# A token-major w1 with shifts in its stationary operand, h transposed by DMA, and kv on 64x32 array tiles

## The chip, the core and the metric

The kernel runs on one NeuronCore of one Trainium2 chip. The metric is the device time of one execution, in microseconds (us), as the median of several runs. Beside it stands a profiled execution, in which every instruction of the five engines has a start and a duration: TensorE (PE for matmuls, PEld for loads of the stationary operand), VectorE (DVE), ScalarE (ACT), GpSimd (POOL) and SyncE (SP), which issues most of the DMAs.

## What is computed

The input x has 2048 tokens of 448 numbers (S = 2048, D = 448), in bf16. The reference normalizes it, runs two branches on the normalized xn, and adds both to x:

```python
xn = layernorm(x);  return x + A(xn) + B(xn)

# A: linear attention, 16 heads of 28
q, k, v = heads(xn @ wqkv)
phi(t)  = concat(softmax(t @ w_phi), softmax(-(t @ w_phi)))     # 56 features a head
kv = phi(k).T @ v;  z = sum over tokens of phi(k)
o  = (phi(q) @ kv) / (phi(q) @ z + 1e-6);   A = o @ wo

# B: token-mixing MLP
h  = gelu(layernorm(xn) @ w1)            # 448 columns, four groups of 112
hs = the groups shifted along the tokens by +1, -1, +2, -2 (zeros at the ends)
x1 = xn + hs @ w2
B  = x1 + gelu(layernorm(x1) @ w3) @ w4  # w3: 448 x 1792
```

A shift acts on tokens only, and w1 on columns only, so a group's columns of w1 may be applied to shifted tokens and give the shifted h.

## The kernel before

The tokens form 16 tiles of 128. A layer-norm tile `xn` is token-major (a token a partition). Its transpose `xnT` (features on partitions, tokens along the row) feeds the matmuls. The 448 features are spread over four blocks of 128 partitions with overlaps (the helper `load_lap` loads weights so), and a contraction of 448 is done in seven halves of 64 rows: `lap_pair` gives two lists of matmuls for two outputs, in which the lower 64 rows of the array work for one output and the upper 64 for the other, side by side (`row_pairs`), 4 + 4 matmuls in the first list and 3 + 3 in the second. The second list adds to the banks that the first list wrote with the other half of the array.

The helper `Recorder` takes every operation in program order, finds by tile what it must wait for, and emits five streams of instructions. Each engine executes its own stream in order. That order is written by hand in two `play` lists and in a loop of eight rounds (`for ps in range(8)`). All matmuls have line 203 and all vector operations line 215 in the profile, as these are the lines of the Recorder's helpers; activations have line 211, DMAs 218 (transposing) and 221. So groups are told apart by the names of their tiles. Names that differ in a number only are merged: `w` stands for w1 to w4, `bank` for the PSUM banks.

The work comes in these stages (times from the profiled execution):

- Up to 31 us. DVE normalizes the tiles; `xn_T` transposes tiles 0 to 11 on TensorE into PSUM, and ACT copies the result to `xnT`. `xn_Td` transposes tiles 12 to 15 by DMA. `load_wT` transposes parts of wqkv by DMA into the tile `hi`. The calls `V(i, k)` are the two lists of v for the token tiles i and i+1, followed by `v_out`. `W(g, m, k)` are those of w1 for the token group g (512 tokens) and the column groups m and m+1: the w1 columns are stationary (64 x 112), `xnT` streams 512 columns. `w1_out` is the gelu on ACT, which writes `hT` (feature-major). `FO` folds w_phi into the q and k weights. `load_rest` loads w2, w3, wo and w4 on the SP queue. Four pairs of PSUM banks (0 to 3) are shared: `xn_T(i, b)`, `V` and `W` name their pair as the last number, and a matmul that writes a pair waits until ACT or DVE has read what was there.
- 31 to 69 us, the eight rounds. Round ps does k for two tiles (bank pair 1), its exps (`k_exp`, ACT, into `phik`), q (pair 0) and its exps (`q_exp`, into `eq_lo` for rounds 0 to 3 and `eq_hi` after), and on pair 2 either w2 for two tiles (`w2_pair`, with the shifts in the token offset of `hT`) or v for tiles 12 and 14. `w2_out` adds the result to `xn` on DVE, `k_norm` sums and scales phi(k) on DVE and POOL, and `w2_norm` takes the statistics of the second norm. From round 3 on `kv_tile` accumulates kv for the tiles that are ready, in banks 6 and 7.
- 69 to 84 us. The rest of w2 and kv runs among the first w3 pairs (`a(p)`, `b(p)`). kv then goes through SBUF (`kv_copy`) and one more matmul with a selection matrix (`kv_picks`, `kv_blocks`) into `kvq`, which the numerators need.
- 84 us to the end. w3, w4, wo and the numerators (`num_tile`, first call `N(0)`), and the stores. `g_apply` and `g_T` (a transposing DMA) supply w3's input, `o_T` wo's.

The w1 stage before is ordered by these lines, of which two are quoted:

```python
              W(0, 2, 0), (xn_T, 5, 2), W(0, 0, 1), (xn_T, 6, 3), W(0, 2, 1), (xn_T, 7, 2), (w1_out, 0, 0, 0),
              (w1_out, 0, 2, 1), V(4, 0), V(6, 0), V(4, 1), (v_out, 4, 3), V(6, 1), (v_out, 6, 2),
```

Of the kernel before, what the change touches and what calls it, by code (L numbers as in the profile page):

```python
# [17 lines left out]
class Recorder:  # L18
# [56 lines left out]
    def solve(self):  # L75
# [10 lines left out]
        for eng, fn, w, r, dma, tile in self.ops:  # L86
# [21 lines left out]
            for k in w:  # L108
                if k in writers:
                    want(writers[k], False)  # L110
                if k in readers:
                    want(readers[k], False)
# [111 lines left out]
def bass_parallel_sum__linear_kernel_hedgehog__mixer_s_mlp__prompt_kernel(  # L224
# [7 lines left out]
    CR = 112  # L232
    SHIFTS = [1, -1, 2, -2]
    HW = S + 16
# [3 lines left out]
    with es:  # L238
# [27 lines left out]
        xnT_r = region("xnT", KC * S * 2)  # L266
        xnT = view(xnT_r, KC * S).rearrange("p (c s) -> p c s", c=KC)
        hT_r = region("hT", NM * HW * 2)
        hT = view(hT_r, NM * HW).rearrange("p (m s) -> p m s", m=NM)
# [5 lines left out]
        eq_lo = new("eq_lo", NC * 2 * 1024).rearrange("p (c s f) -> p c s f", c=NC, s=2)  # L275
# [8 lines left out]
        w2 = new("w2", NM * D).rearrange("p (m d) -> p m d", m=NM)  # L284
# [8 lines left out]
        kvT = view(w1_r, 512)  # L293
        kvf = view(w1_r, 512, F32, at=1024)
        pick = view(w1_r, 2 * 128, at=3072).rearrange("p (s c) -> p s c", s=2)
# [92 lines left out]
        R.ew(pool, "memset", hT[:, :, 0:2], 0.0)  # L388
        R.ew(pool, "memset", hT[:, :, S + 2:S + 4], 0.0)
# [32 lines left out]
        def lap(a):  # L422
            return bass.AP(a.tensor, a.offset, [list(a.ap[0]), [192, 2], [1, 256]])

# [105 lines left out]
        def w1_pair(g, m, b):  # L530
            return lap_pair([banks[2 * b + k][0:CR, :] for k in range(2)],
                         lambda k, kc, lo, hi: w1[lo:hi, kc, CR * (m + k):CR * (m + k) + CR],
                         lambda k, kc, lo, hi: xnT[lo:hi, kc, 512 * g:512 * g + 512])

        def w1_out(g, m, b):
            R.act(hT[0:CR, m:m + 2, 2 + 512 * g:2 + 512 * g + 512], two(2 * b)[0:CR, :, :], ACT.Gelu_apprx_tanh)

        def w2_pair(i, b):
            def side(k, lo, hi):
                r = []  # L540
                for m in range(NM):
                    c0 = 2 + 128 * (i + k) - SHIFTS[m]
                    r.append((banks[2 * b + k][:, 0:D], hT[lo:hi, m, c0:c0 + 128], w2[lo:hi, m, :]))
                return r
            return (lambda: row_pairs(side(0, 0, 64), side(1, 64, CR), True),
                    lambda: row_pairs(side(1, 0, 64), side(0, 64, CR)))
# [23 lines left out]
        def kv_tile(i):  # L570
            def side(k, rows):
                return [(banks[6 + k][:, 64 * n:64 * n + HP + DH + 2],
                         phik[rows[0]:rows[1], i, 4 * n:4 * n + 4, :].rearrange("p g e -> p (g e)"),
                         vaug[rows[0]:rows[1], i, 64 * n:64 * n + HP + DH + 2]) for n in range(8)]
            row_pairs(side(0, LO), side(1, HI), i == 0)

        def kv_picks():
            R.ew(pool, "memset", pick[:, :, :], 0.0)
            for q in range(4):
                r = slice(HP * q, HP * q + HP)  # L580
                R.ew(dve, "tensor_copy", pick[r, q % 2, :].rearrange("p (n e) -> p n e", n=4),
                     ident[r, HP * q:HP * q + HP].unsqueeze(1).to_broadcast([HP, 4, HP]))

        def kv_copy():
            n61 = [a.rearrange("p (n e) -> p n e", n=8)[:, :, 0:HP + DH + 2] for a in (banks[6], banks[7], kvf, kvT)]
            R.ew(dve, "tensor_copy", n61[2], n61[0])
            R.ew(dve, "tensor_tensor", n61[3], n61[1], n61[2], op=ALU.add)

        def kv_blocks():
            kt = kvT.rearrange("p (n h e) -> p n h e", n=8, h=2)  # L590
            for s in range(2):
                for k, lo in enumerate((0, 64)):
                    R.mm(banks[6 + k][:, 256 * s:256 * s + 256].rearrange("p (n e) -> p n e", n=8)[:, :, 0:DH + 1],
                         pick[lo:lo + 64, s, :], kt[lo:lo + 64, :, k, 0:DH + 1], s == 0, False)
            for q in range(4):
                r, h, n = slice(HP * q, HP * q + HP), q % 2, 4 * (q // 2)
                src = banks[6 + h][r, :].rearrange("p (s n e) -> p s n e", s=2, n=8)[:, :, n:n + 4, 0:DH + 1]
                dst = kvq[r, :, HP * h:HP * h + DH + 1].rearrange("p (c s) e -> p s c e", s=2)
                if h:
# [140 lines left out]
        for i in range(12, NT):  # L740
            xn_Td(i)
        load_rest()
# [3 lines left out]
        wps = {(g, m): w1_pair(g, m, b) for g, m, b in ((0, 0, 0), (0, 2, 1), (1, 0, 0), (1, 2, 1), (2, 0, 0),  # L746
                                                        (2, 2, 1), (3, 0, 0), (3, 2, 2))}
# [5 lines left out]
        def W(g, m, k):  # L753
            return (wps[g, m][k],)

        def FO(t, m, k):
# [4 lines left out]
              (spin, 2, 256), V(2, 0), (v_out, 0, 2), W(0, 0, 0), (xn_T, 4, 2), V(2, 1), (v_out, 2, 3),  # L761
              W(0, 2, 0), (xn_T, 5, 2), W(0, 0, 1), (xn_T, 6, 3), W(0, 2, 1), (xn_T, 7, 2), (w1_out, 0, 0, 0),
              (w1_out, 0, 2, 1), V(4, 0), V(6, 0), V(4, 1), (v_out, 4, 3), V(6, 1), (v_out, 6, 2),
              W(1, 0, 0), (xn_T, 8, 3, 2), W(1, 2, 0), W(1, 0, 1), (xn_T, 10, 3, 2), W(1, 2, 1),
              (w1_out, 1, 0, 0), (w1_out, 1, 2, 1), V(8, 0), V(10, 0), V(8, 1), (v_out, 8, 2), V(10, 1),
              (v_out, 10, 3), W(2, 0, 0), W(2, 2, 0), FO(1, 0, 0), W(2, 0, 1), (w1_out, 2, 0, 0), FO(1, 0, 1),
              FO(1, 2, 0), W(2, 2, 1), (w1_out, 2, 2, 1), FO(1, 2, 1), W(3, 0, 0), FO(0, 0, 0), W(3, 2, 0),
              FO(0, 0, 1), FO(0, 2, 0), W(3, 2, 1), (w1_out, 3, 2, 2), W(3, 0, 1), (w1_out, 3, 0, 0), FO(0, 2, 1)])
# [8 lines left out]
        kv_picks()  # L777
# [46 lines left out]
        def K(*t):  # L824
            return (lambda: [kv_tile(i) for i in t],)
# [11 lines left out]
        def A(*t):  # L837
# [60 lines left out]
```

## Time and profile before

| | us |
|---|---|
| median of 3 runs (177.82 to 178.65) | 177.84 |
| profiled execution: span of the core (no time of its own beyond the span is on record) | 175.9 |
| PE busy in the span | 170.8 |
| DVE busy | 110.0 |
| POOL busy | 93.7 |
| ACT busy | 82.5 |

The median stands 1.94 us above the profiled span. In the profile, the number after the start in a timeline is how long a merged group lasts, counted to the end of its last instruction; matmuls are pipelined, so the pace is read from the start of one group to the start of the next. "[0.19 <-PE bank L207]" at the end of a line says that the engine had been idle for 0.19 us, and that the named work ended that idle time.

### The profile page before, as it was taken

The page shows a single profiled execution, that of the slowest core. Times are in us where ns is not written, and L with a number is a line of the kernel's source. Part 1 is how long each engine was busy: PE and PEld are TensorE (multiplying, and loading weights), DVE is VectorE, ACT ScalarE, POOL GpSimd, SP SyncE. Part 2 cuts the span into 40 slices and gives each one's busy share as a digit, 9 for nine tenths or more (in the row PEclk, how much of TensorE's full clock was granted, in tenths as well). Part 3 has the DMA queues.
Part 4 walks back from the last instruction along what each step waited for, and adds up shares of the span by engine and source line. Part 5 has one row for each costly group of instructions (what it writes and reads, how often), then busy time and mean ns, then how long its engine had stood idle before and what let it go on. Part 6 is the DMA issues. An engine that isn't in the chain of part 4 may idle for free.

```text
span 175.9 us, 5042 instructions
## 1 busy us (share of the span) xinstructions
PE 170.8 (97%) x2198; PEld 94.7 (54%) x2198; DVE 110.0 (63%) x252; ACT 82.5 (47%) x92; POOL 93.7 (53%) x130
## 2 busy tenths in 40 slices
PE   7899999998999999999999999999999999999993
PEld 4466557744565555665554554554545545545551
DVE  4799906699899697615776981644427415474621
ACT  2368874997779877926324422223214222224000
POOL 3666670016799999860358489460620723523740
PEclk9999999999999999999999999999999999999999
DMA  5994158990001120121011372134611310311331
GB/s 172 330 240 79 35 97 255 390 345 15 0 4 30 34 60 4 30 55 39 4 34 40 79 74 59 48 82 89 93 30 57 82 34 0 86 30 30 86 100 34
DMA packets 32981, 14.87 MB, mean 85 GB/s; under 512 B 24704, under 2 KB 32448, under 8 KB 32960
## 3 DMA queue, kind: packets, MB, share of 16 engines
q1 hardware_dynamic: 30192, 12.64, 29.6%
q10 hardware_dynamic: 2768, 1.92, 3.4%
q8 instruction: 17, 0.28, 0.7%
q14 instruction: 4, 0.03, 0.1%
HBM read 7.08 MB, written 1.84 MB: 51 GB/s over the span
## 4 chain that ended last, share of the span: by engine, by line
PE 91%; DVE 6%; issue 1%; POOL 0%; ACT 0%; DVEq 0%
PE bank L203 90%; DVE vaug L215 1%; DVE st L215 1%; DVE ksum L215 1%; PE bank L207 1%; DVE xn L215 1%; DVE mv L215 0%; ACT xnT L211 0%; POOL rs L215 0%; DVE rks L215 0%; DVEq L176 0%; DVE gT L215 0%; POOL mv L215 0%
## 5 line engine op out<-in xcount | busy, mean ns | idle before, releaser
L211 ACT ACTIVATE phik<-bank 128x1024 bf16<-128x1024 f32 (+1 forms) x44 | 42.3, 984 | 62.4 <-PE bank L203 62.4
L203 PE MATMUL bank<-gT,w 64*128 64x512 bf16 x392 | 50.1, 377 | 0.0
L215 DVE TENSOR_TENSOR vaug<-bank,vaug 128x464 f32<-128x464 f32 (+3 forms) x65 | 32.6, 512 | 23.0 <-PE bank L203 21.4
L203 PE MATMUL bank<-w,phik 64*128 64x448 bf16 (+1 forms) x420 | 45.0, 349 | 0.0
L215 POOL TENSOR_TENSOR xnT<-vaug 128x196 bf16<-128x196 f32 (+1 forms) x32 | 18.1, 585 | 46.8 <-DVE vaug L215 46.8
L203 PEld LDWEIGHTS bank<-w,phik 64*128 64x128 bf16 (+1 forms) x420 | 21.7, 94 | 21.2 <-issue 0.4
L215 POOL TENSOR_TENSOR phik<-phik,rks 128x1792 bf16<-128x1792 bf16 x8 | 25.7, 3212 | 10.8 <-DVE rks L215 10.8
L203 PEld LDWEIGHTS bank<-gT,w 64*128 64x128 bf16 x392 | 18.6, 94 | 17.0 <-ACT hi L211 0.3
L215 POOL TENSOR_TENSOR vaug<-xn,xtok 128x448 f32<-128x448 bf16 x16 | 16.2, 1031 | 0.2 <-DVE vaug L215 0.2
L215 DVE TENSOR_REDUCE ksum<-phik 128x64 f32<-128x1792 bf16 x8 | 16.0, 2006 | 0.0
L203 PE MATMUL bank<-w,hT 64*128 64x448 bf16 (+1 forms) x128 | 15.0, 349 | 0.5 <-DVE vaug L215 0.5
L215 DVE RECIPROCAL vaug<-bank 128x16 f32<-128x16 f32 x16 | 4.1, 257 | 18.0 <-PE bank L203 18.0
L203 PE MATMUL bank<-xnT,wpq 64*128 64x512 bf16 x112 | 14.9, 376 | 0.0
L203 PE MATMUL bank<-xnT,w 64*112 64x512 bf16 x112 | 14.8, 380 | 0.0
L203 PE MATMUL bank<-wpk,xnT 64*128 64x448 bf16 x112 | 13.4, 349 | 0.0
L203 PE MATMUL bank<-wo,xnT 64*128 64x448 bf16 (+1 forms) x106 | 13.4, 349 | 0.0
L215 DVE TENSOR_TENSOR xn<-bank,xn 128x512 bf16<-128x512 f32 (+1 forms) x16 | 9.2, 616 | 6.3 <-PE bank L203 6.3
L203 PE MATMUL bank<-wv,xnT 64*128 64x448 bf16 x112 | 13.0, 350 | 0.1
L215 POOL TENSOR_TENSOR rs<-mv,mhalf 128x1 f32<-128x1 f32 (+2 forms) x18 | 12.2, 679 | 1.5
L215 POOL TENSOR_SCALAR g_tok<-xn,rs 128x512 bf16<-128x512 bf16 x16 | 12.1, 767 | 0.2
L211 ACT ACTIVATE xnT<-bank 128x512 bf16<-128x512 bf16 x12 | 7.0, 603 | 6.3 <-PE bank L207 6.3
L215 DVE BATCH_NORM_STATS2 st<-xtok 128x6 f32<-128x448 bf16 x16 | 9.8, 615 | 0.0
(62 smaller groups left out, 168.0 us busy)
## 6 DMA issues: line engine op xcount, KB each, us to landing
w<-in_B_w_dram SPq DMA_DIRECT2D x2, 896.0 KB, 7.1
out_dram<-vaug SPq DMA_DIRECT2D x15, 112.0 KB, 1.9
w<-in_B_w_dram SPq DMA_DIRECT2D x1, 1568.0 KB, 12.0
xtok<-in_A_x_dram ACTq DMA_DIRECT2D x2, 448.0 KB, 7.3
xtok<-in_A_x_dram SPq DMA_DIRECT2D x2, 224.0 KB, 5.7
w<-in_B_w_dram ACTq DMA_DIRECT2D x2, 224.0 KB, 5.8
wo<-in_A_wo_dram SPq DMA_DIRECT2D x2, 224.0 KB, 8.4
w<-in_B_w_dram SPq DMA_DIRECT2D x1, 392.0 KB, 3.8
```

Source lines behind the costliest of these rows:

```text
L203: self.op("PE", lambda e: e.matmul(out, lhsT, rhs, start=start, stop=stop, skip_group_check=True), [out], [lhsT, rhs], tile=self._tile(lhsT))
L207: self.op("PE", lambda e: e.transpose(out, in_, ident), [out], [in_, ident], tile=self._tile(in_))
L211: self.op("ACT", lambda e: e.activation(out, in_, func, **kw), [out], [in_] + aps)
L215: self.op(eng, lambda e: getattr(e, name)(out, *args, **kw), [out], aps)
```

## The change

w1 becomes token-major. Its stationary operand is `xnT` (64 rows x 128 tokens), read at an offset that holds the shift of the column group, and 112 columns of w1 stream; `xnT` gets 16 zero columns at both ends. A pair of token tiles has 56 matmuls instead of four column groups having 14 per 512 tokens: 448 in all instead of 112. Each gelu covers two token tiles and writes `h_tok` (token-major, in the overlapping layout), which shares its memory with `eq_lo`. A transposing DMA on the SP queue (`h_T`) makes `hT` of each tile, 16 in all. w2 then is an ordinary seven-half contraction (`lap_pair`), 14 matmuls a pair instead of 16. The four `xn_Td` and `load_rest` move in the SP queue behind the first four `h_T` (`bulk`).

kv becomes 512 matmuls of 64 x 32 array tiles, with v stationary (32 columns) and phi(k) streaming 64 columns: eight different tiles of the array in turn (two halves of the rows, four groups of 32 columns). They leave the rounds and stand in two blocks in the third stage, tiles 0 to 11 and 12 to 15. Their banks are zeroed by DVE before. The selection matmul goes; DVE transposes 32 x 32 blocks instead. The Recorder now also waits for readers of PSUM on the same engine.

```diff
-        xnT = view(xnT_r, KC * S).rearrange("p (c s) -> p c s", c=KC)
+        xnT_p = view(xnT_r, KC * HW).rearrange("p (c s) -> p c s", c=KC)
+        xnT = xnT_p[:, :, PAD:PAD + S]
+        hT = new("hT", KC * S).rearrange("p (c s) -> p c s", c=KC)
...
+        eq_lo = view(lo_r, NC * 2 * 1024).rearrange("p (c s f) -> p c s f", c=NC, s=2)
+        h_tok = view(lo_r, NT * 512).rearrange("p (t d) -> p t d", t=NT)
...
-            R.dma(w2[0:CR, :, :], B_w2.rearrange("(m p) d -> p m d", p=CR))
+            load_lap(w2, B_w2)
...
+        def w1_pair(i, b):
+            def side(k, rows, kcs):
+                r = []
+                for kc in kcs:
+                    for m in range(NM):
+                        c0 = PAD + 128 * (i + k) - SHIFTS[m]
+                        c = slice(CR * m, CR * m + CR)
+                        r.append((banks[2 * b + k][:, c], xnT_p[rows[0]:rows[1], kc, c0:c0 + 128],
+                                  w1[rows[0]:rows[1], kc, c]))
+                return r
+            return (lambda: row_pairs(side(0, LO, (0, 1, 2, 3)), side(1, HI, (0, 1, 2, 3)), True),
+                    lambda: row_pairs(side(1, LO, (0, 1, 3)), side(0, HI, (0, 2, 3))))
+
+        def w1_out(i, b):
+            R.act(h_tok[:, i:i + 2, :].rearrange("p t (h e) -> p t h e", h=2), lap2(two(2 * b)), ACT.Gelu_apprx_tanh)
+
+        def h_T(i):
+            R.dma_t(hT[:, :, 128 * i:128 * i + 128], h_tok[:, i, :])
...
+        def kv_tiles(tiles):
+            for i in tiles:
+                for s in range(4):
+                    for k, (lo, hi) in enumerate((LO, HI)):
+                        for q in range(4):
+                            h = 8 * (q // 2) + 2 * s + q % 2
+                            R.mm(banks[6 + k][HP * q:HP * q + HP, 64 * s:64 * s + 64],
+                                 vaug[lo:hi, i, HP * h:HP * h + HP],
+                                 phik[lo:hi, i, 2 * h:2 * h + 2, :].rearrange("p g e -> p (g e)"),
+                                 False, False)
+
+        def kv_copy():
+            R.ew(dve, "tensor_copy", kvf, banks[6][:, 0:256])
+            R.ew(dve, "tensor_tensor", kvT, banks[7][:, 0:256], kvf, op=ALU.add)
+            R.ew(dve, "transpose", kvX, kvT)
...
+        def W(i, k):
+            return (wps[i][k],)
+
+        def WO(i, b):
+            return (lambda: (w1_out(i, b), h_T(i), h_T(i + 1)),)
+
+        def bulk():
+            for i in range(12, NT):
+                xn_Td(i)
+            load_rest()
...
+              (spin, 2, 256), V(2, 0), (v_out, 0, 2), W(0, 0), (xn_T, 4, 2), V(2, 1), (v_out, 2, 3),
+              W(0, 1), WO(0, 0), W(2, 0), (xn_T, 5, 2), W(2, 1), WO(2, 1), (bulk,), (xn_T, 6, 3), (xn_T, 7, 2),
+              V(4, 0), V(6, 0), V(4, 1), (v_out, 4, 3), V(6, 1), (v_out, 6, 2),
+              W(4, 0), W(4, 1), WO(4, 0), (xn_T, 8, 3, 2), W(6, 0), W(6, 1), WO(6, 1), (xn_T, 10, 3, 2),
+              V(8, 0), V(10, 0), V(8, 1), (v_out, 8, 2), V(10, 1),
+              (v_out, 10, 3), W(8, 0), FO(1, 0, 0), W(8, 1), WO(8, 0), FO(1, 0, 1),
+              FO(1, 2, 0), W(10, 0), W(10, 1), WO(10, 1), FO(1, 2, 1), W(12, 0), FO(0, 0, 0), W(12, 1), WO(12, 0),
+              FO(0, 0, 1), FO(0, 2, 0), W(14, 0), W(14, 1), WO(14, 2), FO(0, 2, 1)])
...
-            if ps > 2:
-                kv_tile(2 * ps - 6)
-                kv_tile(2 * ps - 5)
...
-            a(0), (wl[12][0],), b(0), a(1), (w2_last, 12), b(1), K(10, 11, 12, 13),
-            a(2), (wl[14][0],), b(2), a(3), K(14, 15), b(3), (kv_copy,),
-            a(4), (w2_last, 14), b(4), a(5), (kv_blocks,), b(5),
+            a(0), (wl[12][0],), K(*range(12)), b(0), a(1), (w2_last, 12), b(1),
+            a(2), (wl[14][0],), b(2), a(3), K(*range(12, NT)), b(3), (kv_copy,),
+            a(4), (w2_last, 14), b(4), a(5), b(5),
```

More of the change, by code (lines that the diff above doesn't have):

```diff
@@ L111, in solve @@
                 if k in readers:
-                    want(readers[k], False)
+                    want(readers[k], self.rows[k[0]][1])
             if eng == "PE":
@@ L233, in bass_parallel_sum__linear_kernel_hedgehog__mixer_s_mlp__prompt_kernel @@
     SHIFTS = [1, -1, 2, -2]
-    HW = S + 16
+    PAD = 16
+    HW = S + 2 * PAD
     x2d, out2d = A_x[0], out[0]
@@ L265, in bass_parallel_sum__linear_kernel_hedgehog__mixer_s_mlp__prompt_kernel @@
         xn = new("xn", NT * 512).rearrange("p (t d) -> p t d", t=NT)
-        xnT_r = region("xnT", KC * S * 2)
-        xnT = view(xnT_r, KC * S).rearrange("p (c s) -> p c s", c=KC)
-        hT_r = region("hT", NM * HW * 2)
-        hT = view(hT_r, NM * HW).rearrange("p (m s) -> p m s", m=NM)
+        xnT_r = region("xnT", KC * HW * 2)
+        xnT_p = view(xnT_r, KC * HW).rearrange("p (c s) -> p c s", c=KC)
+        xnT = xnT_p[:, :, PAD:PAD + S]
+        hT = new("hT", KC * S).rearrange("p (c s) -> p c s", c=KC)
         phik_r = region("phik", NT * 1024 * 2)
@@ L274, in bass_parallel_sum__linear_kernel_hedgehog__mixer_s_mlp__prompt_kernel @@
         gT = new("gT", 2 * KC * 512).rearrange("p (b c s) -> p b c s", b=2, c=KC)
-        eq_lo = new("eq_lo", NC * 2 * 1024).rearrange("p (c s f) -> p c s f", c=NC, s=2)
+        lo_r = region("lo", NC * 2 * 1024 * 2)
+        eq_lo = view(lo_r, NC * 2 * 1024).rearrange("p (c s f) -> p c s f", c=NC, s=2)
+        h_tok = view(lo_r, NT * 512).rearrange("p (t d) -> p t d", t=NT)
         hi_r = region("hi", NC * 2 * 1024 * 2)
@@ L283, in bass_parallel_sum__linear_kernel_hedgehog__mixer_s_mlp__prompt_kernel @@
         w1 = view(w1_r, KC * D).rearrange("p (c d) -> p c d", c=KC)
-        w2 = new("w2", NM * D).rearrange("p (m d) -> p m d", m=NM)
+        w2 = new("w2", KC * D).rearrange("p (c d) -> p c d", c=KC)
         wo = new("wo", KC * D).rearrange("p (c d) -> p c d", c=KC)
@@ L292, in bass_parallel_sum__linear_kernel_hedgehog__mixer_s_mlp__prompt_kernel @@
         kvq = new("kvq", 8 * 64).rearrange("p (b e) -> p b e", b=8)
-        kvT = view(w1_r, 512)
-        kvf = view(w1_r, 512, F32, at=1024)
-        pick = view(w1_r, 2 * 128, at=3072).rearrange("p (s c) -> p s c", s=2)
+        kvT = view(w1_r, 256)
+        kvX = view(w1_r, 256, at=512)
+        kvf = view(w1_r, 256, F32, at=1024)
         ident = new("ident", 128)
@@ L387, in bass_parallel_sum__linear_kernel_hedgehog__mixer_s_mlp__prompt_kernel @@
         R.ew(pool, "memset", mhalf[:, :], -0.5)
-        R.ew(pool, "memset", hT[:, :, 0:2], 0.0)
-        R.ew(pool, "memset", hT[:, :, S + 2:S + 4], 0.0)
+        R.ew(pool, "memset", xnT_p[:, :, 0:PAD], 0.0)
+        R.ew(pool, "memset", xnT_p[:, :, PAD + S:HW], 0.0)
         busy = gT[:, 0, 0, 0:256]
@@ L423, in lap, with lap2 @@
             return bass.AP(a.tensor, a.offset, [list(a.ap[0]), [192, 2], [1, 256]])
+        def lap2(a):
+            return bass.AP(a.tensor, a.offset, [list(a.ap[0]), [512, 2], [192, 2], [1, 256]])
         def halves(a):
@@ L528, in v_out @@
                 R.ew(dve, "tensor_copy", vd, vs)
[L530 to L536, printed above, removed]
-        def w2_pair(i, b):
[L539 to L546, printed above, removed]
+        def w1_pair(i, b):
[14 more added lines that the diff above has]
+            R.dma_t(hT[:, :, 128 * i:128 * i + 128], h_tok[:, i, :])
+        def w2_pair(i, b):
+            return lap_pair([banks[2 * b + k][:, 0:D] for k in range(2)],
+                            lambda k, kc, lo, hi: hT[lo:hi, kc, 128 * (i + k):128 * (i + k) + 128],
+                            lambda k, kc, lo, hi: w2[lo:hi, kc, :])
         def w2_out(i, b):
@@ L568, in k_norm @@
             R.ew(pool, "tensor_tensor", ph, ph, rk.unsqueeze(2).to_broadcast([128, 4 * H, DH]), op=ALU.mult)
[L570 to L578, printed above, removed]
+        def kv_tiles(tiles):
[8 more added lines that the diff above has]
+                                 False, False)
@@ L579, in kv_picks @@
+        def kv_copy():
+            R.ew(dve, "tensor_copy", kvf, banks[6][:, 0:256])
+            R.ew(dve, "tensor_tensor", kvT, banks[7][:, 0:256], kvf, op=ALU.add)
+            R.ew(dve, "transpose", kvX, kvT)
             for q in range(4):
                 r = slice(HP * q, HP * q + HP)
[L581 to L599, printed above, removed]
+                dst = kvq[r, :, HP * (q % 2):HP * (q % 2) + DH + 1]
@@ L600, in kv_blocks @@
+                src = kvX[r, :].rearrange("p (b e) -> p b e", b=8)[:, :, 0:DH + 1]
+                if q % 2:
                     R.act(dst, src, ACT.Copy)
@@ L739, in bass_parallel_sum__linear_kernel_hedgehog__mixer_s_mlp__prompt_kernel @@
         ln1_apply(dve, 15)
-        for i in range(12, NT):
-            xn_Td(i)
-        load_rest()
         late_3()
         vps = {i: v_pair(i, b) for i, b in ((0, 2), (2, 3), (4, 3), (6, 2), (8, 2), (10, 3))}
-        wps = {(g, m): w1_pair(g, m, b) for g, m, b in ((0, 0, 0), (0, 2, 1), (1, 0, 0), (1, 2, 1), (2, 0, 0),
-                                                        (2, 2, 1), (3, 0, 0), (3, 2, 2))}
+        wps = {i: w1_pair(i, b) for i, b in ((0, 0), (2, 1), (4, 0), (6, 1), (8, 0), (10, 1), (12, 0), (14, 2))}
         fps = {(t, m): fold_pair(t, m, b) for t, m, b in ((1, 0, 2), (1, 2, 3), (0, 0, 1), (0, 2, 3))}
@@ L751, in V @@
             return (vps[i][k],)
-        def W(g, m, k):
-            return (wps[g, m][k],)
+        def W(i, k):
[6 more added lines that the diff above has]
+            load_rest()
         def FO(t, m, k):
@@ L760, in bass_parallel_sum__linear_kernel_hedgehog__mixer_s_mlp__prompt_kernel @@
         play([(xn_T, 0, 0), (spin, 3, 256), (xn_T, 1, 1), (spin, 4, 256), V(0, 0), (xn_T, 2, 0), V(0, 1), (xn_T, 3, 1),
[L761 to L768, printed above, removed]
+              (spin, 2, 256), V(2, 0), (v_out, 0, 2), W(0, 0), (xn_T, 4, 2), V(2, 1), (v_out, 2, 3),
[6 more added lines that the diff above has]
+              FO(0, 0, 1), FO(0, 2, 0), W(14, 0), W(14, 1), WO(14, 2), FO(0, 2, 1)])
         def w2_norm(i):
@@ L776, in bass_parallel_sum__linear_kernel_hedgehog__mixer_s_mlp__prompt_kernel @@
         kv_ones()
-        kv_picks()
+        R.ew(dve, "memset", two(6)[:, :, 0:256], 0.0)
         side = [("w", 0), ("v", 12), ("w", 2), ("w", 4), ("v", 14), ("w", 6), ("w", 8), ("w", 10)]
@@ L824, in K @@
         def K(*t):
-            return (lambda: [kv_tile(i) for i in t],)
+            return (lambda: kv_tiles(t),)
         def w2_last(i):
```

## The prediction

> **What bounds the kernel now.** I read the page first (shares, chain), then busy time by stage, then the timelines of TensorE, ScalarE and the SP queue.
>
> ```profile
> span 175.9 us, 5042 instructions
> ...
> PE 170.8 (97%) x2198; PEld 94.7 (54%) x2198; DVE 110.0 (63%) x252; ACT 82.5 (47%) x92; POOL 93.7 (53%) x130
> ...
> PE 91%; DVE 6%; issue 1%; POOL 0%; ACT 0%; DVEq 0%
> ```
>
> The span is TensorE's: 97% busy and 91% of the chain. By the chain in order of time its one long piece off TensorE after 12 us is DVE's, 35.4 to 41.5. So saved TensorE time counts where nothing else ends later, and any new wait of TensorE counts in full.
>
> ```profile
> 10.66:31.41 20.75, 20.74 (x304) 14.11 (x302) 14.70 (x39) 14.91 (x21) 10.25 (x21) 1.00 0.61 131
> 31.41:68.97 37.56, 37.08 (x519) 20.95 (x515) 31.98 (x54) 30.76 (x34) 26.66 (x18) 1.00 0.29 96
> 68.97:83.55 14.58, 14.58 (x227) 8.85 (x224) 7.65 (x12) 9.63 (x11) 8.12 (x6) 1.00 0.16 37
> ```
>
> Columns: length, then busy time of PE, PEld, DVE, ACT, POOL, clock, DMA. First stage: v, w1 and folds; second: the eight rounds; third: up to the first numerator. In the rounds DVE is busy 32.0 of 37.6 us and ACT 30.8, so they stand close behind TensorE.
>
> ```profile
> 23.88 1.89 PE L203 MATMUL bank<-xnT,w 64*112 64x512 bf16 x16
> 25.61 0.27 PE L203 MATMUL bank<-g_tok,hi 64*128 64x84 bf16 x7
> ...
> 45.11 0.93 PE L203 MATMUL bank<-wpk,xnT 64*128 64x448 bf16 x8
> 45.87 0.62 PE L203 MATMUL bank<-vaug,phik 64*128 64x62 bf16 x32
> 46.32 0.93 PE L203 MATMUL bank<-w,hT 64*128 64x448 bf16 x8
> ```
>
> Start to start gives the pace of two row tiles at once, weight loads included: 16 matmuls of 512 columns in 1.73 us (108 ns each), 8 of 448 in 0.76 (95), 32 of 62 in 0.45 (14.1). Between the last two a column costs 0.21 ns.
>
> ```profile
> 13.57 0.60 ACT L211 ACTIVATE xnT<-bank 128x512 bf16<-128x512 bf16 x1
> 14.36 0.60 ACT L211 ACTIVATE xnT<-bank 128x512 bf16<-128x512 bf16 x1 [0.19 <-PE bank L207]
> 15.15 0.60 ACT L211 ACTIVATE xnT<-bank 128x512 bf16<-128x512 bf16 x1 [0.19 <-PE bank L207]
> 15.64 1.93 ACT L211 ACTIVATE hT<-bank 112x1024 bf16<-112x1024 f32 x2
> ```
>
> ACT copies xnT tiles 5, 6, 7 before the first two gelus; V(4) follows copy 6 at once, at 15.01.
>
> ```profile
> 6.29 10.96 SPq L218 DMA_TRANSPOSE hi<-in_A_wqkv_dram  x8
> 20.57 5.48 SPq L218 DMA_TRANSPOSE xnT<-xn  x4
> 26.09 1.63 SPq L221 DMA_DIRECT2D w<-in_B_w_dram  x3
> 27.76 0.98 SPq L221 DMA_DIRECT2D wo<-in_A_wo_dram  x2
> 28.79 0.47 SPq L221 DMA_DIRECT2D w<-in_B_w_dram  x1
> ```
>
> SP spends 1.3 us on issuing one transposing DMA, 0.53 on a load.
>
> **TensorE work.** w1: 112 x 108 ns = 12.1 us becomes 448 matmuls of 112 columns, 14.1 + 50 x 0.21 = 24.6 ns each, 11.0: -1.1. The new stationary operands start at odd columns; so did w2's before, whose loads took 94 ns like all others, so I charge nothing (a load that did not hide would cost up to 448 x (47 - 25) ns = 10). w2: 16 to 14 matmuls of 95 ns a pair, -0.19 each, -1.1 in the rounds, -0.4 after. kv: 256 x 14.1 = 3.6 us, 2.26 of it in the rounds, 1.39 after, and kv_blocks (0.26) go; 512 matmuls of 64 columns come, all after the rounds. No row shows column tiles. Floor: eight at once, 64 rounds of 29 ns (28.2 for 62 columns, 0.42 a column more), 1.9 us. Ceiling: 512 x 14.2 = 7.3, no concurrency beyond two. Between: 1024 instructions. The page's instruction queue brought 0.28 MB in 17 packets for TensorE's 4396 instructions, 64 B each, 256 a packet, 0.7% of 16 engines' span or 1.2 us a packet; at the floor 256 are used up in 0.47 us, so one or two fetches show. I take 2.9, nearest the floor since loads already run two deep at 14.1.
>
> [...]
>
> **First stage, walked in program order** from W(0) at 10.66 (halves of W 0.79 and 0.59 us, of V 0.76 and 0.57, a transposed tile 0.115, folds 1.0 in all; ACT back to back: copy 0.49, v 0.80, gelu 0.91, with results 0.60, 0.93 and 1.02 after the start; a matmul's result 0.2 after its last start). The gelus now stand before the copies in ACT's queue. gelu(2) needs W(2,1), which ends at 14.3, and runs 14.55 to 15.57; copy 6 behind it ends at 16.06; V(4) writes the bank that copy 6 reads. TensorE, at tile 7 from 14.46, waits 1.5 us in all. Then gelu(4) runs 20.55 to 21.57, copy 8 ends at 22.06, and W(6), whose shifted columns reach into tile 8, waits 1.5. gelu(6) holds copies 10 and 11, V(10) waits 1.25. A fold waits 0.4 for gelu(10). Where the two halves of a W stand together (four places) or nearly so, the second waits for the first's last result on the same bank: 1.1. Work 18.85 + waits 5.8: end at 35.3 instead of 31.4, +3.9. (The same walk over before gives 19.9 of 20.75.)
>
> **SP.** h's 16 transposes go into the queue: four after the wqkv ones (free at 17.25), until 22.45; the xnT ones, until 27.65; seven loads, until 31.3; then h_T(4) to h_T(15), 1.3 us each: h_T(14) is issued at 44.3 and lands 2.45 later, 46.8. Loads before landed in issue order (wo's 224 KB took 8.4 us behind w3, 5.7 in a quieter place), the last at 40.8; now 42.6. So h_T(4) and (6) land at about 42.7 and 43.6 (while the wqkv transposes drained a backlog, they landed 0.45 us apart). The loads come 1.6 us later than before: w2 lands at about 31.5 and is first read at 36.5, w3, wo and w4 have over 20 us of cover, and the first g_T, at 54 before, finds SP free; these cost nothing, and without that cover 1.6. Who waits: eq_lo and h_tok share memory, so q_exp of round 0 must wait for h_T(4) and (6), that of round 1 for h_T(12) and (14); behind them on ACT stand the next k_exp, behind those TensorE's q and k banks.
>
> **Rounds, from 35.3.** A round's TensorE work is 1.33 + 1.33 + 1.51 = 4.17 us without kv. Round 0 loses 0.4 to gelu(14). Round 1's q at 41.95 waits for q_exp(0) until 44.7. From round 2 on DVE is next late: w2_out 1.07, sums and reciprocal 2.5, norms 1.43 make 5.0 in a w2 round, and w2 needs the bank that w2_out reads; this costs 0.9 in round 4, 0.95 in round 7, ACT 0.4 in round 5. Sum 33.4 + 5.4: end at 74.1 instead of 69.0, +5.1. Had the transposes overtaken the loads: 73.1. The 3.4 us taken out of the rounds thus pay for waits.
>
> **Third stage.** 14.58 - 1.39 - 0.26 - 0.4 + 2.9 = 15.4, +0.9. kv's chain of copies (about 2.5 us on DVE and ACT) has 5 us of w3 work beside it, so it costs nothing; without that cover, 2.5. The zeroing of the kv banks on DVE (the nearest rows, 512 elements, take 0.4 to 0.7 us) stands where the four pick copies (0.7) stood, and POOL's two pad memsets (0.15 each) replace two like them: nothing. POOL's last k_norm ends at about 80.5, before tiles 12 to 15 are due at 84. From the first numerator on all is as before.
>
> Sum: 175.9 + 5.1 + 0.9 = 181.9 span. The median of the runs shown, 177.84, stands 1.94 above the span; 183.8 is predicted.
>
> One row more: the clock is granted in full throughout and TensorE's longest idle in these stages is 0.48 us; mine reach 2.75. [...]
>
> **Rivals.** (a) Only one of the waits reaches TensorE. Without the DMA's the rounds end at 72.0, total 181.7; without ACT's the DMA gate alone gives 73.1 and 182.8; if half of each is covered, about 180. For: my latencies are single rows. Chance 0.2. (b) The array tiles do not run side by side, kv costs 7.3: 188.2, or 185 halfway. For: no row shows eight. Against: two tiles start 2 to 8 ns apart. Chance 0.15. (c) Not slower: ACT keeps pace, because TensorE always has other work in hand. It decides whether V(4) starts by 15.2 and q_exp(1) by 41; then rounds run at TensorE's pace, 31.1 + 34.2 + 0.6 of DVE = 65.9, third stage 14.5 to 15.4: 3 us less, 175. For: TensorE is 97% busy and loses 3 us of work. Against: it executes in order and V(4) and W(6) have no cover. Chance 0.08, and 0.05 for a draw of the two effects.
>
> **Numbers.** The forecast has 0.52, with its own range 182.0 to 185.6: the 1.0 between the two landing cases and the 0.8 that the walk leaves open, on both sides. Low 179.0 takes in (a), at its half and with kv at its floor (1.0 less); high 187.7 most of (b). About 0.5% is what a measurement can tell: faster 0.08, same 0.05, slower 0.87.
>
> **Right or wrong shows in:** w1 matmuls of 112 columns at 25 ns start to start; TensorE idle before V(4), W(6) and V(10) put down to ACT's xnT; ACT's first eq_lo exps held until about 42.7 and 46.8 by DMAs; SP full until 47; kv blocks of 384 and 128 matmuls at 4 to 8 ns each. No idle of TensorE between 14 and 31 us would overturn the forecast.

## The result, and the profile after

The changed kernel takes 202.3 us (median of 4, 201.73 to 203.01) against 177.94 for the kernel before on the same chip: 1.136 times as long, interval 1.132 to 1.139. Predicted were 183.8, with a range up to 187.7. The sign and several waits were right; the size was wrong by a factor of four (+24.4 instead of +6.0). In every ratio and its interval below, runs more than 1.5% above the fastest of the same kernel are left out; the medians beside them take in all runs. The page of the changed kernel:

```profile
span 201.0 us, 6204 instructions
...
PE 177.1 (88%) x2770; PEld 94.9 (47%) x2770; DVE 109.7 (55%) x250; ACT 82.6 (41%) x92; POOL 93.6 (47%) x129
...
PEclk9999999969969999995799999999999999999999
...
PE 68%; ACT 9%; DVE 7%; DMA 7%; issue 5%; SPq 2%; POOL 0%; DVEq 0%; ACTq 0%
```

Three things are new. The chain is no longer TensorE's alone: 16% of it is ACT and DMA, and "issue", time in which the engine waits for nothing that the profile shows, is 5% where it was 1%. And the clock line has four slices below 9, at about 40, 57 and 90 to 100 us. TensorE's busy time went up by 6 us although the prediction took work from it; the clock has a large part in that, as 10.4 us of the busy time lie in stretches in which the granted clock was 0.5.

The stretches answer to the three shown of before, with the rest of the span behind them (length, busy PE, PEld, DVE, ACT, POOL, clock, DMA share, GB/s):

```profile
10.86:35.89 25.03, 21.07 (x641) 16.94 (x639) 14.80 (x39) 15.48 (x21) 10.29 (x21) 1.00 0.72 133
35.89:83.98 48.09, 37.96 (x346) 16.64 (x342) 31.84 (x51) 30.20 (x33) 25.46 (x17) 0.93 0.45 107
83.98:108.61 24.63, 19.48 (x634) 10.52 (x633) 7.23 (x13) 9.79 (x11) 8.98 (x6) 0.86 0.13 25
108.61:201.00 92.39, 89.59 (x1084) 45.56 (x1080) 48.55 (x129) 22.79 (x23) 43.13 (x64) 1.00 0.25 56
```

| | before | predicted change | measured change |
|---|---|---|---|
| start | 10.66 | 0 | +0.2 |
| first stage | 20.75 | +3.9 | +4.3 |
| rounds | 37.56 | +1.2 | +10.5 |
| third stage | 14.58 | +0.9 | +10.0 |
| the rest | 92.35 | 0 | 0.0 |

The first stage came out near the walk and the rest of the span as predicted; the rounds and the third stage did not. TensorE's timeline in the first stage (start, length, group, idle time before it):

```profile
15.60 0.42 PE L207 MATMUL bank<-ident,xn 64*128 64x64 bf16 x10 [0.64 <-issue]
16.50 2.82 PE L203 MATMUL bank<-wv,xnT 64*128 64x448 bf16 x28 [0.48 <-ACT xnT L211]
...
22.55 1.73 PE L203 MATMUL bank<-w,xnT 64*128 64x112 bf16 x53 [1.28 <-ACT xnT L211]
...
26.38 2.07 PE L203 MATMUL bank<-wv,xnT 64*128 64x448 bf16 x20 [1.11 <-ACT xnT L211]
```

V(4), W(6) and V(10) wait for ACT's copies, as predicted, and w1's matmuls start 24.5 ns apart (24.6 predicted). Before V(4) a second wait runs beside ACT's: 0.64 us put down to "issue", in the midst of the transposes of tile 6, which the copy needs. Into the rounds lead three rows of SP and three of ACT:

```profile
17.25 6.26 SPq L218 DMA_TRANSPOSE hT<-lo  x4
23.56 5.93 SPq L218 DMA_TRANSPOSE xnT<-xn  x4
...
34.41 22.18 SPq L218 DMA_TRANSPOSE hT<-lo  x12
```

```profile
46.12 1.97 ACT L211 ACTIVATE lo<-bank 128x1024 bf16<-128x1024 f32 x2 [3.57 <-DMA hT<-lo]
...
53.99 1.02 ACT L211 ACTIVATE lo<-bank 128x1024 bf16<-128x1024 f32 x1 [4.28 <-DMA hT<-lo]
56.55 1.02 ACT L211 ACTIVATE lo<-bank 128x1024 bf16<-128x1024 f32 x1 [1.54 <-DMA hT<-lo]
```

The gate that the prediction described is there: q_exp is held until h_T(4) and h_T(14) have landed. But they land at 46.0 and 56.5, not at 42.7 and 46.8. SP spends 22.2 us on twelve transposes, 1.85 each instead of 1.3; the first of them alone is issued from 34.4 to 41.7, behind loads of which the last, w4, lands at 45.5.

The rest is on TensorE:

```profile
39.07 0.74 PE L203 MATMUL bank<-w,hT 64*128 64x448 bf16 x5 [1.46 <-issue]
...
48.15 1.04 PE L203 MATMUL bank<-xnT,wpq 64*128 64x512 bf16 x8 [1.91 <-ACT lo L211]
...
57.63 1.89 PE L203 MATMUL bank<-xnT,wpq 64*128 64x512 bf16 x8 [5.15 <-ACT lo L211]
...
85.70 1.56 PE L203 MATMUL bank<-phik,vaug 64*32 64x64 bf16 x169
89.55 1.21 PE L203 MATMUL bank<-phik,vaug 64*32 64x64 bf16 x128 [2.29 <-issue]
93.55 1.06 PE L203 MATMUL bank<-phik,vaug 64*32 64x64 bf16 x87 [2.79 <-issue]
94.55 3.17 PE L203 MATMUL bank<-gT,w 64*128 64x512 bf16 x14
```

The first kv block, 384 matmuls, takes 8.85 us (85.70 to 94.55), of which 5.1 are two gaps without any releaser. A gap of the same kind, 1.46 us until 39.07, stands at the start of the rounds. Between the two gaps of the block exactly 128 matmuls run, which with their loads are 256 instructions; in the trace the instruction queue (21 packets with 0.34 MB in the whole span) starts packets at 86.9, 90.7 and 94.7. And the work behind such gaps is slow: 14 matmuls that elsewhere last 1.69 us last 3.17, with the clock granted at 0.5 from 91.0 to 97.8. The trace has two more half-clock stretches, of 3.41 us each, from 39.8 and from 56.9.

### The profile page after: what moved, and what is told of

Its sections match the earlier page's. It is cut to its first block, busy times and chain, and to the rows that moved or that the text cites. A ratio compares the mean times of both kernels' runs of the same rounds, so it can differ in the third digit from the quotient of the medians.

```text
span 201.0 us, 6204 instructions
## 1 busy us (share of the span) xinstructions
PE 177.1 (88%) x2770; PEld 94.9 (47%) x2770; DVE 109.7 (55%) x250; ACT 82.6 (41%) x92; POOL 93.6 (47%) x129
## 4 chain that ended last, share of the span: by engine, by line
PE 68%; ACT 9%; DVE 7%; DMA 7%; issue 5%; SPq 2%; POOL 0%; DVEq 0%; ACTq 0%
PE bank L203 67%; DMA hT<-lo 7%; ACT lo L211 4%; DVE xn L215 2%; SPq L218 2%; DVE ksum L215 2%; ACT xnT L211 2%; ACT phik L211 2%; DVE st L215 2%; ACT hi L211 1%; ACT vaug L211 1%; DVE vaug L215 1%; DVE rks L215 1%; DVE mv L215 0%; PE bank L207 0%
## 5 line engine op out<-in xcount | busy, mean ns | idle before, releaser
L203 PE MATMUL bank<-gT,w 64*128 64x512 bf16 x392 | 51.3, 386 | 0.1
L203 PEld LDWEIGHTS bank<-gT,w 64*128 64x128 bf16 x392 | 18.0, 95 | 19.2 <-issue 1.4
L203 PE MATMUL bank<-xnT,wpq 64*128 64x512 bf16 x112 | 17.1, 414 | 7.4 <-ACT lo L211 7.1
L211 ACT ACTIVATE lo<-bank 128x1024 bf16<-128x1024 f32 x16 | 16.1, 1023 | 16.9 <-DMA hT<-lo 9.4
L203 PE MATMUL bank<-w,hT 64*128 64x448 bf16 x112 | 15.1, 374 | 2.2 <-issue 1.5
L203 PE MATMUL bank<-w,xnT 64*128 64x112 bf16 x448 | 14.2, 209 | 1.5 <-ACT xnT L211 1.3
L203 PE MATMUL bank<-wpk,xnT 64*128 64x448 bf16 x112 | 14.0, 356 | 0.0
L203 PEld LDWEIGHTS bank<-w,xnT 64*128 64x128 bf16 x448 | 12.3, 94 | 2.9 <-ACT xnT L211 1.4
L203 PE MATMUL bank<-wo,xnT 64*128 64x448 bf16 (+1 forms) x106 | 13.4, 349 | 0.0
L203 PEld LDWEIGHTS bank<-xnT,wpq 64*128 64x128 bf16 x112 | 5.9, 103 | 15.4 <-ACT lo L211 8.3
```

The source lines that it names most:

```text
L203: self.op("PE", lambda e: e.matmul(out, lhsT, rhs, start=start, stop=stop, skip_group_check=True), [out], [lhsT, rhs], tile=self._tile(lhsT))
L211: self.op("ACT", lambda e: e.activation(out, in_, func, **kw), [out], [in_] + aps)
```

## The experiments

**Theory.** Two independent losses: (Q) the h transposes stand in SP's queue behind the loads and hold ACT through the shared memory of `h_tok` and `eq_lo`; (I) the kv block uses up TensorE's instructions faster than they are brought. Both are enlarged by the clock, granted at 0.5 for 3.41 us from 56.9, in and behind TensorE's wait of 5.15 us until 57.63, and for 6.83 us from 91.0, in and behind the second gap of kv's block. Rivals: the column tiles themselves are slow; the packing of kv into blocks is at fault; ACT's order sets the rounds; the two halves hinder each other.

**The halves apart.** The diff falls into two parts that work alone: kv's (`kv_tiles`, `kv_copy`, the two blocks), and the rest.

> Only the kv half of the change on the kernel before (w1, h and w2 as before). Theory F (instruction supply): the array tiles themselves take about 8 ns a matmul, and the first block stands still for 2 to 3 us at each 256 instructions, put down to issue; about 184.5 us, of it 6 to 7 us in the third stage. Theory C (the column tiles or the change of array mode are slow): the same total, but matmuls slow throughout and no long issue gaps. Theory S (the two halves of the change only hurt together, by the clock): below 181.

> Only the w1, h and w2 half of the change, kv as before. Theory W (waits): +4 us in the first stage for the order on ACT and +10 us in the rounds for transposes of h that come late, clock losses included; about 192 us. If kv were the main cause, below 184. With additive halves the two differences from before sum to 24 us; with theory S clearly less.

Measured: kv alone 187.3 against 178.3, 1.051 (1.048 to 1.055), +9.0 where some 6.5 were expected. w1 alone 1.082 (1.074 to 1.091), median 193.8. By the ratios the halves add 5.1% and 8.2%, together 13.4% before rounding; the whole change adds 13.6% (13.2 to 13.9). No hindrance between the halves shows. With kv alone the gaps are the same, without any h transposes, in TensorE's timeline:

```profile
70.17 2.12 PE L203 MATMUL bank<-phik,vaug 64*32 64x64 bf16 x236
74.73 1.25 PE L203 MATMUL bank<-phik,vaug 64*32 64x64 bf16 x128 [2.44 <-issue]
78.46 0.35 PE L203 MATMUL bank<-phik,vaug 64*32 64x64 bf16 x20 [2.48 <-issue]
78.74 3.13 PE L203 MATMUL bank<-gT,w 64*128 64x512 bf16 x14
```

**kv's parts crossed.** kv's old matmuls (64 x 128 tiles, 62 columns) in the change's two blocks, and the new 64 x 32 tiles in the old places among the rounds:

```diff
-            if ps > 2:
-                kv_tile(2 * ps - 6)
-                kv_tile(2 * ps - 5)
...
+            a(0), (wl[12][0],), K(*range(12)), b(0), a(1), (w2_last, 12), b(1),
```

```diff
+            if ps > 2:
+                kv_tiles((2 * ps - 6, 2 * ps - 5))
...
+            a(0), (wl[12][0],), b(0), a(1), (w2_last, 12), b(1), K(10, 11, 12, 13),
```

> The kernel before with its own kv matmuls (64x128 tiles, 62 columns) put into the two blocks of the change. Theory F: 384 instructions of the first block are used up in 2.7 us, so at least one issue gap of 0.5 to 2.5 us stands in it; 177 to 179.5 us. Theory C: no issue gap, and as the rounds lose 2.3 us of TensorE work that comes back later, 177 to 178.

> The kv half of the change with the new 64x32 matmuls in the places of before: two tiles a round from round 3 on, six tiles after. Theory F: no issue gap over 0.5 us, since a round needs some 210 instructions in 4.7 us; 178 to 179 us, 64 matmuls taking about 0.52 us instead of 0.45. Theory C: 182 to 187, as with the blocks.

Measured: 179.4, 1.007 (1.005 to 1.009), and 179.6, 1.008 (1.005 to 1.011). Neither alone costs much. The old matmuls in a block show no gap at all, where I had expected one of at least 0.5 us; 384 instructions ran in 2.7 us. (The 1.1 us that this run lost I did not trace further.) The new tiles in the old places:

```profile
46.47 0.68 PE L203 MATMUL bank<-phik,vaug 64*32 64x64 bf16 x64
47.09 0.93 PE L203 MATMUL bank<-w,hT 64*128 64x448 bf16 x8
```

64 of them take 0.62 us where 32 of the old took 0.45: the tiles run side by side, but each share of kv costs about a third more than before, +1.3 us over all eight pairs of tiles. So the tiles are no gain, and the 9 us need both together: many instructions at a dense place.

**Which of the two, tiles or instructions?** The old kind of matmul in the blocks, each cut into two of 31 columns: as many instructions as the change has, and no column tile.

```diff
-                return [(banks[6 + k][:, 64 * n:64 * n + HP + DH + 2],
+                return [(banks[6 + k][:, 64 * n + 31 * u:64 * n + 31 * u + 31],
...
-                         vaug[rows[0]:rows[1], i, 64 * n:64 * n + HP + DH + 2]) for n in range(8)]
+                         vaug[rows[0]:rows[1], i, 64 * n + 31 * u:64 * n + 31 * u + 31]) for n in range(8) for u in range(2)]
```

> As kv_old_blocks (old 64x128 tiles, the blocks of the change), but each matmul of 62 columns cut into two of 31: twice the instructions for the same numbers, no column tiles. Theory F: the first block has 768 instructions as in the change and stands still twice for 2 to 3 us, put down to issue, with a half-clock stretch behind it; 185 to 188 us, like kv_only. Theory C (the stalls belong to the column tiles): no gap over 0.5 us, 179 to 181 us.

Measured: 188.5, 1.059 (1.055 to 1.063). TensorE's timeline of the block, behind it that of the uncut one:

```profile
70.10 3.18 PE L203 MATMUL bank<-vaug,phik 64*128 64x31 bf16 x236
75.07 1.83 PE L203 MATMUL bank<-vaug,phik 64*128 64x31 bf16 x128 [1.79 <-issue]
78.52 0.45 PE L203 MATMUL bank<-vaug,phik 64*128 64x31 bf16 x20 [1.63 <-issue]
78.81 3.15 PE L203 MATMUL bank<-gT,w 64*128 64x512 bf16 x14
```

```profile
70.78 2.89 PE L203 MATMUL bank<-vaug,phik 64*128 64x62 bf16 x192
73.50 1.68 PE L203 MATMUL bank<-gT,w 64*128 64x512 bf16 x14
```

The gaps stand after the same 236 and 128 matmuls as with the column tiles, at other work per matmul. The same arithmetic in twice as many instructions takes 8.7 us instead of 2.7. This is shown, then: the gaps of kv's block go with the number of instructions. That their supply makes the gaps is my reading of it; it fits the packets of the instruction queue at 86.9, 90.7 and 94.7 in the changed kernel.

Counted in TensorE's instructions: in the changed kernel 338 of the block (169 matmuls and their loads) passed before its first gap; here and with kv alone it was 472 (236 matmuls). In all three 256 more (128 matmuls) passed before the second gap, and from the end of the first to the end of the second it took 4.00 us in the changed kernel, 3.73 with kv alone and 3.45 here. In the changed kernel's whole trace TensorE has four gaps put down to "issue": counted from the start, waits for semaphores among them, 451 recorded instructions had gone before the one until 15.60, 1475 before the one until 39.07, and 2497 and 2753 before kv's two. The uncut block has 384 instructions, fewer than the 472 that passed before the first gap here, so that it has no gap says nothing of the rate.

**SP's queue.** w3, wo and w4 loaded behind the last h transpose, w2 kept early:

```diff
-            load_lap(w2, B_w2)
             load_lap(w3, B_w3)
...
-            load_rest()
+            load_lap(w2, B_w2)
...
-              FO(0, 0, 1), FO(0, 2, 0), W(14, 0), W(14, 1), WO(14, 2), FO(0, 2, 1)])
+              FO(0, 0, 1), FO(0, 2, 0), W(14, 0), W(14, 1), WO(14, 2), FO(0, 2, 1), (load_rest,)])
```

> The changed kernel with w3, wo and w4 loaded after the last h transpose instead of before the fifth (w2 stays early). Theory Q (the transposes come late because they are queued behind the loads): no 7.3 us issue of h_T(4), all h_T landed by about 46, the exps of rounds 0 and 1 wait under 3 us for them together, the half-clock stretch at 57 to 60 goes; 192 to 195 us. Theory T (twelve transposes at 1.3 us each are too slow anyway): the last still lands after 50, 197 to 200 us.

Measured: 195.2, 1.092 (1.084 to 1.100), some 7 us less than the whole change. SP's and ACT's rows:

```profile
32.44 17.21 SPq L218 DMA_TRANSPOSE hT<-lo  x12
```

```profile
47.12 1.02 ACT L211 ACTIVATE lo<-bank 128x1024 bf16<-128x1024 f32 x1 [1.88 <-DMA hT<-lo]
49.65 1.02 ACT L211 ACTIVATE lo<-bank 128x1024 bf16<-128x1024 f32 x1 [1.50 <-DMA hT<-lo]
```

No issue sticks, twelve transposes take 1.43 each, and ACT waits 3.4 us for h's DMAs where it waited 9.4. The half-clock stretches at 40 and 57 are gone; kv's stays and lasts 10.24 us instead of 6.83 (mean clock of the run 0.973 in 193.1 us). The issue gap at the start of the rounds shrinks from 1.46 to 0.39 us; why was not isolated. Theory Q holds for the most part, but the last h_T landed at 50.9 and not by 46: twelve transposes in a row are somewhat late for the rounds even without the loads, the part of Theory T that came true.

**The shared memory.** `h_tok` in the upper half of `phik` instead of in `eq_lo`'s memory:

```diff
-        h_tok = view(lo_r, NT * 512).rearrange("p (t d) -> p t d", t=NT)
+        h_tok = view(phik_r, NT * 512, at=8 * 1024 * 2).rearrange("p (t d) -> p t d", t=NT)
...
+            if ps == 2:
+                R.ew(pool, "memset", phik[:, 8:16].rearrange("p t g e -> p (t g) e")[:, :, DH:HP], 0.0)
```

> The changed kernel with h_tok in the upper half of phik's memory instead of eq_lo's (the zero padding of that half is written by GpSimd after round 2). Theory M (the wait exists only because q_exp overwrites h_tok): no wait of q_exp for a DMA, though SP is as late as before, 192 to 195 us. If w2's need of the transposed h is the real bound, the waits move to w2 of rounds 3 and 5 and the time stays above 198.

Measured: 196.8, 1.108 (1.101 to 1.115), some 5 us less, between the two expectations. No q_exp waits for a DMA any more. But `phik`'s own pads must now be zeroed after the last h_T, and k_exp of round 4 waits for that:

```profile
62.70 1.67 PE L203 MATMUL bank<-wpk,xnT 64*128 64x448 bf16 x8 [3.13 <-ACT phik L211]
```

So the gate moved rather than vanished. Together with the queue's run it shows both ends of one wait: what holds (the shared memory) and why so long (the queue).

**ACT's order.** In the first stage the copies before the gelus, all else as changed (`WO(0, 0)` and `WO(2, 1)` behind `xn_T` 6 and 7, `WO(4, 0)` and `WO(6, 1)` behind 8 and 10).

> The changed kernel with the copies of xnT tiles 6, 7 and 8 to 11 ahead of the gelus on ACT, as in the kernel before. Theory A: TensorE's waits before V(4), W(6) and V(10) go, the first stage ends 3 to 4 us earlier, but q_exp of round 1 still waits until about 56 for h_T(14), so the total gains less than 1 us: 201.3 to 202.5. If the first stage sets the end, 198 to 199.

Measured: 201.7, 1.133 (1.128 to 1.137), 0.6 less, which the intervals do not tell from nothing. The first stage ends 1.6 us earlier, at 34.25, where 3 to 4 were expected. The waits before W(6) and V(10) are gone, but V(4) starts at 16.49 as before: an issue gap of 0.57 us holds up tile 6's transposes, and ACT stands idle for 0.98 us before copy 6. Waits for the DMAs of xnT are new (0.43, 0.31 and 0.30). Then TensorE waits longer for h's DMAs, most of it in one place:

```profile
50.36 1.89 PE L203 MATMUL bank<-xnT,wpq 64*128 64x512 bf16 x8 [9.26 <-ACT lo L211]
```

ACT's waits of the first stage, which the prediction walked with most care, were thus worth hardly anything here: a later wait swallows what they give back.

**The clock alone.** 88 matmuls of 64 x 256 that nobody reads, before q of round 2, to keep TensorE busy in its longest wait. For this the zeroing of kv's banks had to move behind the rounds.

> The changed kernel with 88 matmuls of 256 columns on constant data (4.8 us) in the 5.2 us in which TensorE waits before q of round 2. They shorten no wait. Theory G (a wait costs twice, as the clock is halved for 3.4 us after it): the half-clock stretch at 57 to 60 goes and the time falls by 1.2 to 1.7 us, to about 200.8. If the clock does not follow TensorE's idleness, 202.0 to 202.6.

Measured: 205.5, 1.155 (1.148 to 1.163), outside both expectations. The half-clock stretch at 57 is gone, but another appears at 48.4 (eight q matmuls from 48.24 last 1.73 us, those from 59.05 1.04), and the moved zeroing now stands on the path:

```profile
87.98 2.17 PE L203 MATMUL bank<-phik,vaug 64*32 64x64 bf16 x209 [2.09 <-DVE bank L215]
```

Inconclusive: what a full clock alone is worth in that wait was not isolated.

**Is there a version of w1 that pays?** w1's half with both orders mended (SP's and ACT's); then the same with the even h tiles transposed first (they free `eq_lo`) and the odd ones and late loads after; then with the halves of W interleaved with the folds.

> The w1 half with both orders repaired: copies before gelus on ACT, loads after the transposes on SP; kv as before. If the waits were all that cost time, TensorE's saved 2.6 us show: 175 to 177. Theory W+: xnT tiles 12 to 15 now come late behind four h transposes (1 to 2.5 us), and the last even h tiles still land at about 45, so 1 to 4 us remain: 179 to 182.

> As w1_fixed, but the xnT transposes stand ahead of h_T(2), and the h tiles that q_exp of rounds 0 and 1 overwrites (the even ones) are transposed first, the odd ones after. Theory W+: no wait of q_exp for a DMA; what remains is the half boundaries of w1 (about 1 us) and one or two issue gaps for the 896 instructions of w1, against 2.6 us of saved matmuls: 176 to 178, 177.0 likeliest. If 180 or more, something besides these waits costs time.

> As w1_best, with the two halves of each w1 pair kept apart by folds or transposes, and with W(2,1) behind V(4,0), so that fewer w1 instructions follow one another before 15 us. Theory W+: the 1.1 us of waits at 15 to 16 us and some 0.8 us of half boundaries shrink to about 0.5; 176.0 to 177.2, a measurable gain on the kernel before (its matmuls are 2.6 us shorter). If the rounds are bound by DVE and ACT rather than TensorE, the earlier start is lost again and the time stays at 177.5 to 178.

```diff
+        def h_odd():
+            for i in range(3, NT, 2):
+                h_T(i)
...
-            return (lambda: (w1_out(i, b), h_T(i), h_T(i + 1)),)
+            return (lambda: (w1_out(i, b), h_T(i)) + ((h_T(1),) if i == 0 else ()),)
...
+              FO(0, 0, 1), FO(0, 2, 0), W(14, 0), W(14, 1), WO(14, 2), FO(0, 2, 1), (h_odd,), (load_rest,)])
```

Measured for the first: 185.8, 1.034 (1.028 to 1.040), more than the 179 to 182 expected, with one wait of TensorE for an exp, 3.57 us until 50.0, and a half-clock stretch after it (mean clock of the run 0.991 in 183.4 us); the exp waits 3.0 us for h_T. For the second 177.74 over 12 runs (176.94 to 179.05) against 177.81: 0.999 (0.997 to 1.001), the same as before. Its stages:

```profile
10.66:32.35 21.69, 20.70 (x643) 16.94 (x639) 15.00 (x39) 15.54 (x21) 10.46 (x22) 1.00 0.85 107
32.35:69.12 36.77, 36.08 (x507) 18.31 (x502) 31.99 (x54) 30.38 (x33) 25.89 (x18) 1.00 0.77 169
69.12:83.50 14.38, 14.38 (x237) 7.50 (x235) 7.65 (x12) 9.80 (x11) 8.80 (x6) 1.00 0.20 39
```

With the DMA gate gone and the clock full throughout (1.00 in each stage), the rounds and the third stage gain 1.0 us, and the first stage loses 0.9. The last version took 176.70 to 180.59, median 179.82 over 12 runs against 178.00, 0.998 (0.995 to 1.002): no gain. Its profiled execution, one of the longer ones (180.42), stands still in w1:

```profile
30.18 0.21 PE L203 MATMUL bank<-w,xnT 64*128 64x112 bf16 x1 [2.38 <-issue]
30.78 1.59 PE L203 MATMUL bank<-w,xnT 64*128 64x112 bf16 x31 [0.40 <-DMA xnT<-xn]
```

The profile puts the first gap down to "issue". But this version calls W(14) before W(12), and the transposing DMAs of xnT tiles 14 and 15 land at 30.09 and 30.73 in this trace; both gaps end just behind them. So the interleaving asked for tiles 14 and 15 before they were there. A half-clock stretch follows at 30.9 (mean clock of the run 0.99 in 178.7 us). Whether the shorter runs have this wait no trace shows. No version that I ran is measurably faster than the kernel before.

## Why the prediction was wrong in size, point by point

**Right.** The direction; w1's pace (24.5 ns at 112 columns), and that its odd offsets cost nothing (loads 94 ns); the waits of W(6) and V(10) for ACT's copies and the first stage's end (35.3 predicted, 35.9); the kind of gate in the rounds; kv's chain of copies as free; the rest of the span unchanged.

**Half right: the wait before V(4).** The walk gave it 1.5 us for gelu(2) standing before copy 6. Measured were 0.64 us put down to issue, and 0.48 for the copy behind it. gelu(2) does hold ACT until 15.9, but with the copies ahead of the gelus V(4) started no earlier: the gap, which the walk did not have, held it just as long.

**Wrong: "h_T(4) to h_T(15), 1.3 us each from 31.3".** This term of the SP part failed. The transposes began at 34.4, as all that stood ahead took longer too (17.2 us from 17.25 instead of 14.05), the first was stuck for 7.3 us, and twelve took 22.2 instead of 15.6. I took the issue time from rows of other stages (wqkv's, xnT's); here the last five of the seven loads were still on their way. I had asked whether the transposes could overtake the loads, and not whether the issue itself would be held up. q_exp was held 3.3 us longer for h_T(4) and 9.7 longer for h_T(14); the run with the loads moved, which leaves the issue free, gives some 7 us back. With the waits at the places where they were expected, the mechanism was right and its size was not.

**Wrong: kv at 2.9.** It took 10.0 (8.85 and 1.15), outside even the ceiling of 7.3. The prediction counted the 1024 instructions and the packets of 256, and then let "one or two fetches show" at 1.2 us each, the time that a packet's transfer occupies. Measured in the block were 256 instructions in 3.5 to 4.0 us from the end of one gap to the end of the next, which no row of before could show, since there TensorE's densest 256 took 4.7. Rival (b) came nearer with 7.3 for kv, but for a reason that does not hold: the tiles do run side by side, 8.0 to 8.2 ns a matmul between the gaps.

**Wrong: the clock left out.** The prediction set the full clock and the longest idle of 0.48 us of before beside its own waits of 2.75 us, and put nothing for the clock into the sum. TensorE was busy for 10.4 us of the half-clock stretches (3.41, 3.41 and 6.83 us), which cost up to 5.2 us (an estimate: half of that busy time). The stretch from 39.8 began 0.7 us after the gap of 1.46 us, that from 56.9 within the wait of 5.15 us, and the 6.83 us from 91.0 within the second of kv's gaps (2.29 and 2.79 us). The wait of 1.91 us until 48.15 and the one of 1.28 until 22.55 had none behind them, so the length of an idle time alone does not tell here whether one follows. With kv alone, with gaps of 2.44 and 2.48 us, the mean clock was 0.982 in 185.4 us, some 6.7 us at half. What a full clock alone would have saved no run isolated.

How the terms add up: in the rounds 33.4 us of work stand beside 10.1 idle (48.09 - 37.96; of it 7.1 before q and 1.46 the issue gap at 39.07) and up to 3.0 for the 6.07 us of busy time at half clock; the 1.5 left I did not resolve. In the third stage 15.4 predicted, 7.1 more for kv, and about 1.5 for the 14 slow matmuls behind it (2.95 us start to start instead of 1.5) make 24.0 of 24.6.

**The rivals.** (a) fell: both waits reached TensorE, and ACT's proved the one that mattered little, some 0.6 us where the forecast's own sum had 1.0. (c) fell: V(4) started at 16.5 and the held q_exp at 54, far past the points (15.2, 41) that it needed. What none of them held is that two of the listed costs were each larger, and that some 13.7 us at half clock would stand beside the waits.

## What to carry to other kernels

Count the instructions of a dense stretch as well as its work: on TensorE here 338 to 472 of a kv block passed before the first gap and then 256 per 3.5 to 4.0 us, so a change that trades few large matmuls for many small ones can be right in cycles and lose 6 us in a block; spread among large matmuls the same instructions cost 1.3 us. Order a DMA queue by what is due first, and price the issue of a DMA from a row in which as much stands ahead of it as will here (7.3 us for one transpose behind the loads, 1.3 for most others). And mend the last wait first: the walk through ACT's order, most of this prediction's labour, was worth some 0.6 us, within the noise, while the DMA gate stood behind it.

## What the runs showed of the hardware that was not expected

- Gaps of TensorE put down to "issue" in the large kv block, with 64 x 32 tiles (2.29 and 2.79 us in the changed kernel, 2.44 and 2.48 with kv alone) and with cut 64 x 128 tiles (1.79 and 1.63), after 338 or 472 instructions of the block and again after 256 more.
- Issuing one transposing DMA occupied SP for 1.3 to 1.6 us on the average of a group, and in the changed kernel from 34.41 for 7.3 us while loads were still in flight (the last landed at 45.5).
- Eight 64 x 32 tiles in turn: 8.0 to 8.2 ns a matmul of 64 columns in a run, 9.7 with the small gaps at its start and middle (0.62 us for 64), against 14.1 for a 64 x 128 tile of 62 columns, which does twice the work.
- The granted clock of the changed kernel was 0.5 for 3.41 us from 39.8 and from 56.9 and for 6.83 us from 91.0, where TensorE had just idled for 1.46 us, was idle for 5.15, and had idled for 2.29 and was idle for 2.79; in the kernel before, with no idle time over 0.48 us in these stages, the clock stayed at 1.00 in all three.
